# The 2738 pieces of a sparse-attention and SwiGLU kernel issued in another order

## Chip, core and metric

One Trainium2 chip, one of its cores. The time is the device time of one execution in microseconds (us); lower is better. Of the kernel before, three runs and one profiled execution are given.

## What is computed

Block-sparse attention over B=4 sequences, H=8 heads, S=768 positions and D=64, in blocks of 32 positions, followed by a gated feed-forward layer on the 3072 tokens:

```python
mask = np.abs(blk_i - blk_j) <= window            # window = 1
mask = mask | (blk_i == 0) | (blk_j == 0) | (blk_i == n_blocks - 1) | (blk_j == n_blocks - 1)
...
mask[qb * block:(qb + 1) * block, kb * block:(kb + 1) * block] = True   # 3 drawn blocks per row block
scores = np.where(mask, scale * np.matmul(q, k.transpose(0, 1, 3, 2)), -1000000000.0)
attn = softmax(scores); x = attn @ v              # then heads side by side: (3072, 512)
g = x @ w_gate; silu = g * (1.0 / (1.0 + np.exp(-g)))
out = silu * (x @ w_val) @ w_out                  # 512 -> 1536 -> 512
```

So a row block of 32 queries sees its own three neighbouring key blocks, the two edge blocks (first and last) and three blocks whose numbers come from a table in memory. The first and the last row block see all keys.

## The kernel before

The tokens go through in nine chunks (`CHUNKS`): three of 256 tokens, which are batch 0, and six of 384, two for each of batches 1 to 3. The first two chunks run in fp32, the others with every fp32 number split into two fp16 halves and products of three terms. The feed-forward products (L1811 and L1817 into 1536 columns, L1882 back to 512) are most of TensorE's work; attention for later chunks is done between them.

Nothing in the kernel is scheduled by a planner at run time. Every step of the work is a `Task`, made by `Plan.add` with its engine, the tasks that it needs and the buffers that it takes. `Plan.order` walks through the list `TURN` (L48), 2738 task numbers, asserts that each stands behind what it needs, and hands them out in that order; each task then emits its instructions. An engine works through its own instructions in that order and no other. So `TURN` alone decides what an engine does next, and an instruction that waits holds up everything behind it on its engine.

What the prediction speaks of lies in the start-up, on batch 0, whose row blocks go in pairs (`pair0`; "pair 1" below is row blocks 1 and 2, "pair 3" row blocks 3 and 4, and so on: the digit in a tile's name such as `qk_3_0` is the first row block of the pair). For one pair:

- SP's queue loads the table of drawn blocks (L328), three parts of k (L584), three parts of v (L619), the last block of v (L626) and the queries (L1342, L1348). DVE turns the table into numbers (`tables`, L364 to L366 and `rows`, L360). POOL and DVE each load these numbers into registers in pieces of eight row blocks (TENSOR_LOAD, L1111, from `koff`).
- TensorE transposes k (L593); DVE and ACT keep it (L600, L602).
- `keys` copies the drawn key blocks side by side (L1402 and L1404: DVE for the first chunk's two first pairs, POOL for all the other ones), `beside` the neighbouring blocks (L1411, ACT or POOL). Slots are reused, so the copies for a later pair wait until an earlier pair's scores are done.
- the value blocks go into one of six places of `w2all`: the edge blocks by `spread` (L630: one copy on ACT, three on DVE, once for all six places), the neighbouring blocks by `values` (L1429, ACT or DVE), the drawn blocks by `gathered` (L1433: an indirect DMA that POOL issues).
- `scores` on TensorE (L1452, and L1468 for repeated blocks), `top` on DVE (L1474), `power` on ACT (L1484, the exponentials), `turn` on TensorE (L1492), `turned` (L1498, DVE or ACT, to SBUF), `product` with the values (L1512), `scaled` (L1520), `x_turn` (L1529), `x_put` (L1580).

The weights come by SP in pieces (L472) and are decoded on DVE (L450 to L452). In batches 1 to 3 the transposition is a DMA (L1258, `pts<-pp`), and the product is L1270.

Of the kernel before, what the change touches and what calls it, by code (L numbers as in the profile page):

```python
# [48 lines left out]
    2, 60, 7, 5, 0, 6, 18, 1, 3, 129, 23, 303, 22, 16, 21, 36, 28, 29, 84, 219, 38, 4, 8, 9, 19, 40, 20, 10, 14, 11,  # L49
    27, 15, 17, 88, 12, 13, 43, 46, 45, 44, 47, 30, 69, 66, 62, 63, 42, 68, 65, 86, 220, 67, 224, 26, 301, 24, 90,  # L50
    48, 91, 89, 70, 112, 49, 50, 71, 72, 41, 52, 51, 54, 53, 92, 73, 55, 93, 25, 111, 94, 114, 113, 56, 39, 74, 225,
    31, 95, 57, 75, 79, 32, 96, 58, 134, 137, 136, 135, 37, 97, 76, 77, 78, 33, 64, 115, 138, 110, 116, 117, 159,
    158, 80, 98, 139, 157, 160, 81, 140, 118, 100, 120, 119, 141, 142, 124, 99, 179, 85, 182, 102, 87, 107, 221,
    101, 59, 61, 161, 162, 164, 108, 130, 109, 122, 163, 131, 103, 165, 121, 123, 222, 143, 180, 302, 133, 181, 104,
    153, 202, 145, 223, 147, 132, 183, 154, 105, 106, 184, 82, 83, 186, 185, 187, 204, 234, 125, 226, 126, 227, 228,
    203, 235, 144, 146, 166, 127, 229, 201, 230, 205, 309, 148, 168, 206, 149, 188, 308, 128, 447, 155, 208, 156,
    190, 167, 169, 207, 448, 209, 236, 199, 237, 171, 238, 449, 450, 176, 175, 178, 170, 172, 200, 451, 279, 151,
    244, 245, 210, 34, 35, 189, 191, 457, 177, 192, 150, 330, 310, 280, 212, 231, 152, 232, 311, 198, 233, 307, 313,
    197, 239, 312, 173, 193, 214, 240, 194, 281, 174, 458, 211, 213, 215, 314, 283, 282, 246, 247, 195, 216, 248,
    459, 331, 196, 217, 332, 218, 541, 460, 542, 543, 284, 452, 319, 461, 333, 241, 304, 305, 335, 334, 464, 242,  # L60
    466, 249, 250, 315, 467, 336, 317, 316, 243, 465, 468, 269, 337, 327, 462, 306, 463, 318, 544, 285, 545, 471,
    286, 251, 328, 453, 473, 474, 320, 338, 469, 347, 339, 326, 252, 472, 340, 348, 349, 350, 351, 329, 359, 470,
    341, 342, 353, 321, 322, 475, 323, 354, 476, 360, 401, 361, 355, 253, 270, 356, 397, 271, 477, 324, 325, 478,
    364, 362, 366, 357, 343, 480, 481, 254, 370, 365, 272, 546, 344, 400, 367, 551, 479, 273, 368, 371, 372, 553,
    382, 383, 373, 374, 384, 385, 396, 376, 377, 255, 256, 257, 258, 422, 423, 378, 264, 379, 482, 402, 380, 554,
    345, 363, 265, 287, 483, 484, 292, 288, 387, 389, 291, 403, 552, 388, 424, 425, 404, 405, 426, 406, 485, 399,
    390, 486, 555, 289, 487, 391, 266, 684, 407, 267, 556, 557, 1011, 488, 259, 260, 398, 290, 892, 454, 489, 408,
    492, 490, 268, 494, 495, 409, 261, 262, 274, 275, 410, 493, 263, 496, 491, 893, 346, 437, 352, 497, 498, 558,
    559, 560, 561, 562, 565, 548, 566, 547, 438, 276, 896, 293, 277, 278, 411, 439, 298, 432, 572, 563, 564, 567,
# [116 lines left out]
    2669, 2670, 2680, 2681, 2682, 2676, 2677, 2685, 2683, 2686, 2684, 2687, 2688, 2689, 2692, 2693, 2694, 2699,  # L186
    2700, 2695, 2690, 2691, 2696, 2697, 2698, 2706, 2707, 2701, 2702, 2703, 2704, 2714, 2715, 2716, 2708, 2705,
    2709, 2710, 2711, 2712, 2717, 2718, 2720, 2721, 2722, 2719, 2723, 2726, 2724, 2725, 2727, 2728, 2729, 2732,
    2730, 2731, 2733, 2734, 2735, 2736, 2737,
]  # L190


# [1788 lines left out]
```

## Time and profile before

| | |
|---|---|
| runs of before | 756.51, 758.19, 758.41 us; median 758.19 |
| the profiled execution | 756.43 us, of it a span of 754.2 us from the first to the last instruction |
| granted TensorE clock, mean | 0.988 |
| TensorE (PE) | 724.6 us busy, 96% |
| VectorE (DVE) | 546.9 us, 73% |
| ScalarE (ACT) | 471.4 us, 63% |
| GpSimd (POOL) | 236.6 us, 31% |
| chain of work that ended last | PE 80%, DVE 10%, DMA 3%, ACT 2%, issue 2% |

The profile is of one execution. An engine's busy time is the time in which it works on an instruction, its own waits for a port among them; the idle time of the engine that is busy almost throughout is what another order could remove. The granted clock is the share of full speed that TensorE was given.

### The profile page before, as it was taken

The page shows a single profiled execution, that of the slowest core. Times are in us where ns is not written, and L with a number is a line of the kernel's source. Part 1 is how long each engine was busy: PE and PEld are TensorE (multiplying, and loading weights), DVE is VectorE, ACT ScalarE, POOL GpSimd, SP SyncE. Part 2 cuts the span into 40 slices and gives each one's busy share as a digit, 9 for nine tenths or more (in the row PEclk, how much of TensorE's full clock was granted, in tenths as well). Part 3 has the DMA queues.
Part 4 walks back from the last instruction along what each step waited for, and adds up shares of the span by engine and source line. Part 5 has one row for each costly group of instructions (what it writes and reads, how often), then busy time and mean ns, then how long its engine had stood idle before and what let it go on. Part 6 is the DMA issues. An engine that isn't in the chain of part 4 may idle for free.

```text
span 754.2 us, 23313 instructions
## 1 busy us (share of the span) xinstructions
PE 724.6 (96%) x9207; PEld 452.3 (60%) x9207; DVE 546.9 (73%) x1570; ACT 471.4 (63%) x1123; POOL 236.6 (31%) x290
## 2 busy tenths in 40 slices
PE   4779999999999999999999999999999999999998
PEld 3447788884588456645665456645665556545655
DVE  6898999887999988556999677756878466723310
ACT  4698685787878776764887575655766555522221
POOL 3695412132124351220343222321334232302210
PEclk8799999999999999999999999999999999999999
DMA  8656567655799999987899999797758856540001
GB/s 279 193 167 222 174 229 246 203 175 116 186 180 187 183 191 167 192 262 134 189 201 176 219 204 202 184 177 165 168 124 177 165 122 112 92 82 29 0 1 43
DMA packets 182429, 122.91 MB, mean 163 GB/s; under 512 B 131728, under 2 KB 152592, under 8 KB 182320
## 3 DMA queue, kind: packets, MB, share of 16 engines
q1 hardware_dynamic: 176688, 104.12, 60.6%
q0 software_dynamic: 5632, 17.31, 9.6%
q8 instruction: 72, 1.18, 0.7%
q14 instruction: 37, 0.30, 0.1%
HBM read 79.31 MB, written 11.01 MB: 120 GB/s over the span
## 4 chain that ended last, share of the span: by engine, by line
PE 80%; DVE 10%; DMA 3%; ACT 2%; issue 2%; SPq 1%; DVEq 0%; POOL 0%; ACTq 0%; POOLq 0%
PE p L1817 38%; PE po L1882 22%; PE p L1811 9%; PE pv L1270 3%; PE qk L1203 3%; DMA w2all<-in_v_dram,vidx 1%; PE pv L1512 1%; DVE w2all L1429 1%; PE qkf L945 1%; PE pvf L1033 1%; SPq L762 1%; DVE e L1217 1%; DMA pts<-pp 1%; PE qk L1452 1%; DVE w1t L413 1%
## 5 line engine op out<-in xcount | busy, mean ns | idle before, releaser
L1817 PE MATMUL p<-xall,w1t 128*128 128x384 f16 (+1 forms) x2016 | 321.9, 319 | 0.1
L1817 PEld LDWEIGHTS <-w1t 128*128 128x128 f16 x2016 | 193.5, 98 | 118.2 <-issue 5.7
L1841 POOL TENSOR_TENSOR h<-act,h 128x384 f16<-128x384 f32 (+1 forms) x108 | 100.3, 930 | 319.6 <-ACT h L1838 319.3
L1882 PE MATMUL po<-w2all,h 128*128 128x512 f16 (+1 forms) x900 | 191.4, 371 | 1.2 <-issue 1.2
L1882 PEld LDWEIGHTS <-h 128*128 128x128 f16 x900 | 86.4, 98 | 96.6 <-issue 2.3
L1185 POOL DMA_INDIRECT w2all<-vd,vidx x66 | 65.0, 985 | 84.8 <-PE pv L1270 64.2
L1824 ACT ACTIVATE act<-p,gsc 128x384 f32<-128x384 f32 (+1 forms) x84 | 46.8, 559 | 65.5 <-PE p L1817 51.1
L1811 PE MATMUL p<-xall,w1t 128*128 128x256 f32 x384 | 86.6, 384 | 0.4 <-DVE act L1833 0.4
L1838 ACT CAST h<-act 128x384 f16<-128x384 f32 (+1 forms) x108 | 50.7, 470 | 51.5 <-DVE act L1833 51.1
L1828 DVE SCALAR_TENSOR_TENSOR act<-act,p 128x384 f32<-128x384 f32 (+1 forms) x108 | 54.4, 505 | 36.9 <-ACT act L1824 35.8
L1236 ACT ACTIVATE e<-e,mx,es 128x256 f32<-128x256 f32 x132 | 78.2, 593 | 2.2
L1811 PEld LDWEIGHTS p<-xall,w1t 128*128 128x128 f32 x384 | 72.3, 192 | 10.3 <-DVE act L1833 0.7
L1833 DVE SCALAR_TENSOR_TENSOR act<-act,hs,p 128x384 f32<-128x384 f32 (+1 forms) x84 | 49.4, 590 | 14.3 <-PE p L1817 12.2
L413 DVE SCALAR_TENSOR_TENSOR pp<-e,pp 128x512 f16<-128x512 f32 x66 | 48.3, 734 | 10.4 <-ACT pp L410 10.2
L1217 DVE CUSTOM_DVE_ANT_1 e<-qk,msk 128x256 f32<-128x256 f32 x132 | 49.5, 418 | 7.4 <-PE qk L1203 7.4
L1175 DVE COPY kring<-kst 128x256 f16 x198 | 40.2, 256 | 4.2 <-PE qk L1203 2.6
L1755 POOL TENSOR_TENSOR sqx<-sqx 128x768 bf16<-128x768 bf16 (+3 forms) x18 | 22.2, 1232 | 66.9 <-ACT sqx L1751 58.7
L410 ACT ACTIVATE pp<-e 128x512 f16<-128x512 f32 x66 | 40.7, 622 | 3.2 <-DMA pts<-pp 2.8
L1709 ACT ACTIVATE ot<-po,oc 128x512 f32<-128x512 f32 (+1 forms) x25 | 16.3, 659 | 25.8 <-PE po L1882 25.7
L1203 PE MATMUL qk<-kring,qs 64*32 64x256 f16 x1584 | 29.3, 271 | 1.5 <-DVE kring L1176 1.0
L1270 PEld LDWEIGHTS <-pts 128*32 128x32 f16 x2112 | 24.1, 97 | 10.6 <-issue 9.4
L1433 POOL DMA_INDIRECT w2all<-in_v_dram,vidx x22 | 24.5, 1112 | 18.8 <-DVE vidx L360 10.3
(205 smaller groups left out, 917.0 us busy)
## 6 DMA issues: line engine op xcount, KB each, us to landing
stage<-in_w_dram SPq DMA_DIRECT2D x36, 512.0 KB
w2all<-vd SPq DMA_DIRECT2D x66, 192.0 KB
out_dram<-ot SPq DMA_DIRECT2D x19, 256.0 KB
qn<-in_q_dram SPq DMA_DIRECT2D x36, 128.0 KB
stage<-in_v_dram SPq DMA_DIRECT2D x9, 512.0 KB
qraw<-in_q_dram SPq DMA_DIRECT2D x36, 128.0 KB
vd<-stage SPq DMA_DIRECT2D x9, 512.0 KB
stage<-in_k_dram SPq DMA_DIRECT2D x9, 512.0 KB
```

What stands on the lines that cost most here:

```text
L413: nc.vector.scalar_tensor_tensor(lo, src, scale, hi, op0=ALU.mult, op1=ALU.subtract)
L1185: nc.gpsimd.indirect_dma_start(vf[0:96, 1, :], None, bt.vd, bass.IndirectOffsetOnAxis(ap=vidx[0:96, qb : qb + 1], axis=0))
L1203: nc.tensor.matmul(st[g][u * BLK : (u + 1) * BLK], o.q[half, ql, u, col : col + BLK], kg[half, 4 * kl + u].rearrange("p s k -> p (s k)"), ...
L1217: nc.vector.tensor_tensor_reduce(ev[:, g], score_of(g).rearrange("p (s k) -> p s k", k=BLK), o.g.msk[:, qb, :].unsqueeze(2).broadcast_to([ ...
L1236: nc.scalar.activation(ev[:, g], ev[:, g], AF.Exp, bias=nb_[:, g : g + 1], scale=o.g.es[:, 0:1], accum_out=both["rs"][:, n % 2, g : g + 1],)
L1811: nc.tensor.matmul(t[:, 0:tc_], w[:, i + 1, k_ * P : (k_ + 1) * P], x_k(k_), start=k_ == 0, stop=k_ == NKT - 1)
L1817: nc.tensor.matmul(t[:, 0:tc_].rearrange("p (s q) -> p s q", q=BLK), w_[:, f, m, k_, :], x_k(k_, l), start=i == 0, stop=i == 11)
L1828: nc.vector.scalar_tensor_tensor(a_, a_, 1.0, pg.tile[:, 0:tc_], op0=ALU.add, op1=ALU.mult)
L1833: nc.vector.scalar_tensor_tensor(a_, a_, sc, pw.tile[:, 0:tc_], op0=ALU.mult, op1=ALU.mult)
L1838: nc.scalar.copy(hv(f)[:, 0, :], act.tile[:, 0:tc_])
L1841: nc.gpsimd.tensor_tensor(hv(f)[:, 1, :], act.tile[:, 0:tc_], hv(f)[:, 0, :], op=ALU.subtract)
L1882: nc.tensor.matmul(po.tile[:, cs], hv(f)[:, l, ts_], w2h[:, f, m, cs], start=f == 0 and i == 0, stop=f == NF - 1 and i == 2)
```

## The change

Only the list `TURN` differs: the same 2738 numbers, permuted. Its first row before and after (the other rows differ in the same manner):

```diff
 TURN = [
-    2, 60, 7, 5, 0, 6, 18, 1, 3, 129, 23, 303, 22, 16, 21, 36, 28, 29, 84, 219, 38, 4, 8, 9, 19, 40, 20, 10, 14, 11,
...
+    0, 5, 8, 2, 60, 10, 1, 7, 22, 3, 9, 6, 18, 4, 21, 23, 28, 29, 16, 11, 303, 19, 14, 38, 15, 20, 17, 12, 13, 44,
...
```

No instruction is added or taken away but those that set registers and semaphores. Three places of the start-up, as the program has them on their engines:

**SP's first transfers.** Before:

```order
L328 DMA xall<-in_sampled_blocks_dram 128x144
L584 DMA w1t<-in_k_dram 128x2x512 x3
L626 DMA w2all<-in_v_dram 32x512
L619 DMA w2all<-in_v_dram 128x2x512
L1348 DMA q_0_174<-in_q_dram 64x4x128 x2
```

and after:

```order
L584 DMA w1t<-in_k_dram 128x2x512
L328 DMA xall<-in_sampled_blocks_dram 128x144
L584 DMA w1t<-in_k_dram 128x2x512
L619 DMA w2all<-in_v_dram 128x2x512
L584 DMA w1t<-in_k_dram 128x2x512
L1348 DMA q_0_161<-in_q_dram 64x4x128 x2
L626 DMA w2all<-in_v_dram 32x512
```

The table of drawn blocks now stands behind a part of k, the third part of k behind a part of v, and the last block of v behind the first queries.

**DVE and POOL around the first scores.** On DVE, from the copy of the edge values to the first transposed probabilities, before:

```order
L630 COPY w2all<-w2all 32x3x512
L1474 TENSOR_REDUCE mx_1_320<-qk_1_0_271 128x2
L1474 TENSOR_REDUCE mx_1_320<-qk_1_1_272 128x2
L1474 TENSOR_REDUCE mx_3_355<-qk_3_0_326 128x2
L1474 TENSOR_REDUCE mx_3_355<-qk_3_1_327 128x2
L1429 COPY w2all<-w2all 32x512
L1429 COPY w2all<-w2all 64x512
L1498 COPY pts_1_1_373<-pt_1_1_367 128x512
L630 COPY w2all<-w2all 32x3x512
L1474 TENSOR_REDUCE mx_5_406<-qk_5_0_382 128x2
```

and after:

```order
L630 COPY w2all<-w2all 32x2x512
L1429 COPY w2all<-w2all 32x512
L1429 COPY w2all<-w2all 64x512
L1474 TENSOR_REDUCE mx_1_332<-qk_1_0_232 128x2
L1474 TENSOR_REDUCE mx_1_332<-qk_1_1_233 128x2
L1474 TENSOR_REDUCE mx_3_345<-qk_3_0_265 128x2
L1474 TENSOR_REDUCE mx_3_345<-qk_3_1_266 128x2
L1111 TENSOR_LOAD koff
L630 COPY w2all<-w2all 32x3x512
L1498 COPY pts_1_1_395<-pt_1_1_355 128x512
L630 COPY w2all<-w2all 32x3x512
L1474 TENSOR_REDUCE mx_5_422<-qk_5_0_402 128x2
```

The two copies of neighbouring values (L1429) now stand ahead of the tops (L1474), the two larger edge copies (L630) behind them, and a register load that stood far later in the program stands in between. On POOL at the same time, before:

```order
L1111 TENSOR_LOAD koff x3
L1433 DMA w2all<-in_v_dram,vidx 96x512 x6
L1404 REGISTER_ALU
L1404 ISA
L1404 COPY w1t<-kst_233 128x4x32
```

and after:

```order
L1111 TENSOR_LOAD koff
L1433 DMA w2all<-in_v_dram,vidx 96x512
L1111 TENSOR_LOAD koff
L1433 DMA w2all<-in_v_dram,vidx 96x512
L1111 TENSOR_LOAD koff
L1433 DMA w2all<-in_v_dram,vidx 96x512 x2
L1411 COPY w1t<-kst_142 128x4x96 x2
L1404 REGISTER_ALU
```

Four gathers instead of six now stand ahead of the key copies, each of the first three behind a register load of its own. On TensorE the product of pair 1 (L1512, 32 columns of `pv_1`) moved behind the transposes of pair 3 and the scores of pair 7; before it stood ahead of both.

**POOL ahead of the product of batch 0's second chunk.** Before, from the key copies for chunk 2 (`kring`) on:

```order
L1402 COPY kring_104<-kst_233 128x8x32
L1404 REGISTER_ALU
L1404 ISA
L1404 COPY kring_104<-kst_233 128x4x32
L1404 REGISTER_ALU x2
L1404 ISA
L1404 COPY kring_104<-kst_233 128x4x32
L1404 ISA
L1404 COPY kring_104<-kst_233 128x4x32
L1433 DMA w2all<-in_v_dram,vidx 96x512
L1755 TENSOR_TENSOR sqx_909<-sqx_909 128x512
```

and after:

```order
L1433 DMA w2all<-in_v_dram,vidx 96x512 x3
L1755 TENSOR_TENSOR sqx_874<-sqx_874 128x512
L1755 TENSOR_TENSOR sqx_874<-sqx_874 128x256
L1433 DMA w2all<-in_v_dram,vidx 96x512 x2
L1402 COPY kring_104<-kst_142 128x8x32
L1404 REGISTER_ALU
L1404 ISA
L1404 COPY kring_104<-kst_142 128x4x32
```

The gather that stood behind both groups of key copies is now the second of the three in a row ahead of the second group. Further on, the gather that stood behind both additions of squares (L1755) of the next chunk now stands between them. In the rest of the program TensorE's tasks move by at most six places within its own order, and the feed-forward products at the end stay nearly as they were.

## Rows read from the trace of the kernel before

**Rows 1.** Page, busy time, share of the span and instructions.

```profile
PE 724.6 (96%) x9207; PEld 452.3 (60%) x9207; DVE 546.9 (73%) x1570; ACT 471.4 (63%) x1123; POOL 236.6 (31%) x290
```

**Rows 2.** Waits of TensorE: total us, times, longest.

```profile
PE pv L1512 <- DVE pts L1498: 4.1, 1, 4.1
...
PE pv L1512 <- DMA w2all<-in_v_dram,vidx: 2.8, 2, 1.9
```

**Rows 3.** Busy time by stretch: engines (instructions), then clock, DMA share, GB/s.

```profile
0.00:20.00 20.00, 10.19 (x98) 6.41 (x98) 13.92 (x54) 8.82 (x18) 7.56 (x16) 0.83 0.90 284
...
40.00:60.00 20.00, 14.38 (x367) 10.64 (x365) 18.51 (x33) 19.70 (x51) 18.64 (x31) 0.93 0.55 180
...
260.00:660.00 400.00, 397.09 (x5413) 226.29 (x5412) 292.58 (x919) 257.07 (x615) 123.73 (x121) 1.00 0.84 173
```

**Rows 4.** Timeline of DVE, 0 to 37: start, length, idle before in brackets.

```profile
4.55 0.20 DVE L364 SCALAR_TENSOR_TENSOR koff<-xall 128x24 int32<-128x24 int32 x1 [2.52 <-DMA xall<-in_sampled_blocks_dram]
...
12.02 0.69 DVE L630 COPY w2all<-w2all 32x1024 f32<-32x1024 f32 x1
...
16.73 1.22 DVE L630 COPY w2all<-w2all 32x1536 f32<-32x1536 f32 x1
17.88 2.46 DVE L1474 TENSOR_REDUCE mx<-qk 128x2 f32<-128x512 f32 x4
20.36 6.79 DVE L1429 COPY w2all<-w2all 32x512 f32<-32x512 f32 x2
27.19 0.69 DVE L1498 COPY pts<-pt 128x512 f32<-128x512 f32 x1
...
34.01 1.99 DVE L1474 TENSOR_REDUCE mx<-qk 128x2 f32<-128x512 f32 x3 [0.24 <-PE qk L1468]
```

**Rows 5.** Line L1429: ns of one copy, minimum, median, maximum.

```profile
L1429 DVE COPY w2all<-w2all x8: 420/423/6357, 20.4 to 41.3; 32x512 f32<-32x512 f32 x4, 64x512 f32<-64x512 f32 x4
```

**Rows 6.** Timeline of POOL, 7 to 82.

```profile
11.52 1.30 POOL L1433 DMA_INDIRECT w2all<-in_v_dram,vidx  x1 [10.27 <-DVE vidx L360]
...
19.45 0.75 POOL L1404 COPY w1t<-kst 128x128 f32 x3
20.16 0.50 POOL L1411 COPY w1t<-kst 128x384 f32<-128x384 f32 x1
...
25.69 0.76 POOL L1404 COPY w1t<-kst 128x128 f32 x3
...
48.77 2.77 POOL L1404 COPY kring<-kst 128x128 f32 x3
51.70 0.95 POOL L1433 DMA_INDIRECT w2all<-in_v_dram,vidx  x1 [0.16 <-PE pv L1512]
...
71.91 2.24 POOL L1755 TENSOR_TENSOR sqx<-sqx 128x512 bf16<-128x512 bf16 x2 [7.54 <-ACT sqx L1749]
```

**Rows 7.** Lines L1111 and L1433: ns of one register load; us from gather to landing.

```profile
L1111 POOLq TENSOR_LOAD <-koff x3: 1395/1824/2032, 5.2 to 8.8; - x3
L1111 DVEq TENSOR_LOAD <-koff x3: 1857/2097/2905, 5.2 to 185.4; - x3
...
DMA to landing us min/median/max: 3.1/5.5/8.1
```

**Rows 8.** Timeline of TensorE.

```profile
16.20 0.56 PE L1468 MATMUL qk<-dupm,ones_h 128*128 128x192 bf16 x4
...
57.27 1.08 PE L1512 MATMUL pv<-w2all,pts 128*32 128x64 f32 x32 [1.86 <-DMA w2all<-in_v_dram,vidx]
...
79.53 0.99 PE L1512 MATMUL pv<-w2all,pts 128*32 128x64 f32 x56 [0.94 <-DMA w2all<-in_v_dram,vidx]
...
406.11 0.52 PE L1270 MATMUL pv<-w2all,pts 128*32 128x128 f16 x32 [0.39 <-DMA pts<-pp]
```

**Rows 9.** Page, DMA issues: transfer, queue, count, KB each.

```profile
w2all<-vd SPq DMA_DIRECT2D x66, 192.0 KB
```

280 rows, old and new, of the table TURN are left out of this document.

## Prediction

> **What bounds the kernel now.** I read the busy times first. TensorE is busy for 724.6 us of the span of 754.2 [rows 1], so no order can give back more than 29.6 us without making TensorE's own work shorter, and the change adds or removes no work. The table by stretch says where these 29.6 us lie: between 260 and 660 us TensorE is busy for 397.09 of 400, while the first 60 us are far from full, 10.19 of 20 in the first stretch and 14.38 of 20 in the third [rows 3]. The reader is to see there that the third stretch is also one in which ACT works 19.70 and DVE 18.51 of 20: start-up is bound by these two engines and by what they wait for. Then I read TensorE's waits. The largest behind the loading of k is 4.1 us, for the transposed probabilities of the first product, and two waits for gathered values make 2.8 us [rows 2].
>
> The DVE timeline shows the cause of the first. A copy of neighbouring values, 32 partitions by 512, begins at 20.36 and with its sister takes 6.79 us [rows 4]. The same copy takes 0.42 us as a rule, and 6.36 here [rows 5]. On POOL, key copies run from 19.45 to 26.44 without a gap [rows 6], and DVE's copy ends 0.28 us behind them. So such a copy on DVE, from SBUF to SBUF in fp32, stands still as long as POOL goes from copy to copy. The transposed probabilities (27.19) stand behind it. This is the row on which the forecast turns, since the change moves the very copies that can be caught.
>
> **The change, part by part.** All sums are made against the profiled execution, 756.43 us.
>
> *The table behind a part of k.* DVE gets the table's numbers at 4.55 [rows 4]. The table now stands behind a transfer of 512 KB (128 partitions of two rows of 512 fp32). At the 284 GB/s of the first stretch [rows 3] that takes 1.85 us. The table can come later by nothing (if its own latency covers it) up to about 1.85 and one more issue on SP of 0.5, in all 2.3 us. I take 1.1, the middle, because no row shows a small transfer behind a large one. Everything on DVE and POOL that reads the table shifts by this. In return the edge copy of 0.69 us, which stood ahead of the key copies at 12.02, now stands behind them [rows 4]. The key copies thus end 0.4 us later, at 17.15 where they ended at 16.73, and the first scores at 17.2 where they ended at 16.76 [rows 8].
>
> *When POOL begins its key copies.* Before, POOL did three register loads, then six gathers in 7.93 us (11.52 to 19.45), so 1.32 each [rows 6]. After, three loads of 1.82 [rows 7] and four gathers of 1.32 come first: 5.5 and 5.3 us from about 6.3 (the table's 5.2 and the shift), so until 17.1. The slots that the key copies write come free with the first scores at 17.2. POOL starts there, 2.2 us earlier than before.
>
> *DVE's copies meet that run.* DVE does its edge copy from 17.15 to 17.84, and the two copies of neighbouring values want to follow. POOL has asked by then. Does DVE get in? In the row of before it did not, for all the 6.1 us that POOL's run still had. I take the same: POOL's run of two copies of L1411, twelve of L1404 and two of L1411, at 0.5 and 0.25 us each [rows 6], makes 5.0 us, until 22.8. The value copies end at 23.6, and the four tops, 2.46 us [rows 4], at 26.1 instead of 20.34. That is a loss of 5.8 us there, but the product of pair 1 no longer stands in front of the scores that follow.
>
> *The rest of the start-up on DVE.* The register load that came from later in the program takes 2.1 us [rows 7], until 28.2; the edge copy 1.22 [rows 4], until 29.4; the transposed probabilities 0.69 [rows 4], until 30.1. The second edge copy meets POOL's next run, which waits for the scores of pair 5 and the first edge copy, and takes 0.75 for three copies, twice, and 1.0 for two of the others, 2.5 us [rows 6], until 31.9; the copy ends at 33.1. Two tops (half of 2.46) and the small inverses behind them, which I put at 0.3, make 1.5 us, one more copy of probabilities 0.69, and the tops of pair 7 start at 35.3 instead of 34.01 [rows 4]. These tops release ACT's exponentials, and from 40 on ACT has hardly a gap [rows 3]. **+1.3 us**. If POOL lets the copies through at once, the same sum is 5.0 and 1.8 us shorter and the tops start at 28.5 or so: 5.4 us earlier. These are the two ends: −5.4 and, with the table 1.2 us later than I take, +2.5.
>
> The Trainium skill, page "SBUF — State Buffer", section "SBUF: two separate sides", says that DVE and GpSimd share one port pair under a lock which whoever starts first holds for the whole instruction. By that sentence a DVE copy would wait for the one POOL copy under way; the row of 6.36 us shows a wait for a whole run of them, so the measurement is the worse of the two. By the page's lock alone this part would come out near the first rival's −4.4 us; by the row it is the +1.3 above.
>
> *The gather for the second chunk's product.* TensorE waits 1.86 us at 57.27 [rows 8] for a gather issued at 51.70, right behind a group of key copies whose last three took 2.77 [rows 6]. It lands 5.5 us after its issue [rows 7], which is 57.2. Now it is issued ahead of that group, so at least 2.77 earlier, with the shift of 1.3 near 50.2, and lands at 55.7; the product's first half ended at 55.41, where the wait began, and now ends behind that, shifted too. **−1.9 us**; nothing if ACT, which writes the rest of that product's input, turns out to be as late as the gather.
>
> *The gather of the third chunk.* TensorE waits 0.94 us at 79.53 [rows 8]. The gather stood behind two additions of squares that take 2.24 together [rows 6] and now stands behind one, about 1.1 earlier. What is late next is the second addition and the norms that need it, now behind a gather; TensorE's feed-forward products stand ahead of these. **−0.9 us**, bounds −0.9 and +1.3, one gather's worth of delay for those norms.
>
> *The rest.* Between 260 and 660 us TensorE lacks 2.9 us in all [rows 3]. Of these, one product that waited 0.39 us for its transposed probabilities [rows 8] now stands behind one more feed-forward group, which covers it: **−0.4 us**. Moves of up to six places elsewhere I cost at nothing; what hides them is TensorE's queue of feed-forward work. Bounds: −2.9, and a loss that the third rival prices. TensorE's clock I also cost at nothing: it is granted at 0.83 on the mean of the first stretch, so for a part of it at 1.2 GHz, and at the full 2.4 GHz in the long middle [rows 3]; the start-up has idle TensorE time before and after.
>
> *Sum.* +1.3 − 1.9 − 0.9 − 0.4 = −1.9, so 754.5 against 756.43. The three runs and the profiled execution, four times in all, have their middle at 757.35, 0.9 above the profiled one. The same 0.9 on top gives **755.4 us** for a median, against 758.19.
>
> **The rivals.** *The copies get through* (chance 0.25). A copy of DVE that asks at the end of its own copy keeps the port, or waits for one POOL copy. For it: DVE is the one at work when POOL arrives. Against it: the 6.36 us [rows 5]. Four such copies that each wait for one POOL copy of 0.5 us cost 2.0 of the 5.4 us, so the start-up gains between 3.4 and 5.4, say 4.4, and the sum is −4.4 − 1.9 − 0.9 − 0.4 = −7.6: 748.8, and 749.7 for a median.
>
> *ACT and DVE take it all back* (chance 0.16). With 19.70 and 18.51 busy of 20 [rows 3], what the gathers give and what the lock costs may both end in the same queue of work, and the first product of the feed-forward layer then starts when it did. Only −0.4 and a third of −0.9 are left: 755.7, and 756.6 for a median. In effect, nothing changes.
>
> *Slower, by fetches that come late in the long middle* (chance 0.14). In batches 1 to 3 every product needs probabilities that a DMA has transposed, from a queue with a DMA share of 0.84 [rows 3], and one such wait of 0.39 us is all there is now. Where the new order puts one more transfer of 192 KB [rows 9] ahead of such a transposition, it lands 1.1 us later (192 KB at 173 GB/s, rows 3). If that falls once in each of the six chunks on a product with no feed-forward work ahead of it, it costs 6.6 us: +1.3 − 1.9 − 0.9 + 6.6 = +5.1, so 761.5 and 762.4 for a median. It decides as soon as a landing comes later than TensorE's work between; for it speaks that SP's order there is changed nearly throughout, against it that most moves are by two places or fewer.
>
> **How the numbers follow.** My forecast has 0.45. Its own range is 751.8 to 758.5: down by the table's 1.1 and the 2.5 us that the long middle still holds, up by the table's 1.2 and the first gather's 1.9. About 0.3%, 2.3 us, is what a measurement here can tell from no change: 755.9 to 760.5 is the same. Of the forecast's 0.45, 0.27 are below that and 0.18 in it; the first rival lies below (0.25); of the second 0.02 lie below, 0.13 in it and 0.01 above; the third is above. So 0.54 faster, 0.31 same, 0.15 slower. The range, 748.8 to 760.5, takes in the first rival (748.7 to 750.7 by its own bounds) but for its last tenth, and leaves out the third.
>
> **What would show it.** In the profile after: the table's first row on DVE near 5.6; POOL's copies from about 17.3; one or both copies of L1429 near 5 us long, ending where POOL's first run ends, and an edge copy (L630) of about 3 us; the tops of pair 7 near 35; no wait of TensorE above 0.5 us for gathered values at 55 to 60 and at 79. If all copies of L1429 and L630 take 0.4 to 1.2 us, the first rival holds. If TensorE's busy share between 260 and 660 falls below 396 of 400 with waits for `pts<-pp`, the third does. The forecast is wrong if TensorE's idle time in the first 80 us changes by more than 5 us.

## The result, and the profile after

The kernel after takes 750.54 us (median of four executions, 748.77 to 751.29) against 757.88 for four of the kernel before (756.51 to 758.41). The ratio is 0.9908, with a 95% interval of 0.9882 to 0.9934: 7.3 us faster, where 2.8 were forecast (755.4 against 758.19). The time lies in the whole range that was given, 748.8 to 760.5, but below the forecast's own part of it, 751.8 to 758.5, and beside the first rival, 749.7. Four of all executions below, at 848 to 1242 us, fell in a slower state and are left out of medians and ratios.

The profiled execution after is the longest of the four, 751.29 us with a span of 749.1, so the two profiles differ by 5.1 us only. First the busy times of the profile after, and two lines of each page, before and then after:

```profile
PE 721.9 (96%) x9207; PEld 452.3 (60%) x9207; DVE 542.9 (72%) x1570; ACT 473.9 (63%) x1123; POOL 237.0 (32%) x290
...
L1817 PE MATMUL p<-xall,w1t 128*128 128x384 f16 (+1 forms) x2016 | 321.9, 319 | 0.1
L1882 PE MATMUL po<-w2all,h 128*128 128x512 f16 (+1 forms) x900 | 191.4, 371 | 1.2 <-issue 1.2
...
L1817 PE MATMUL p<-xall,w1t 128*128 128x384 f16 (+1 forms) x2016 | 321.1, 319 | 0.0
L1882 PE MATMUL po<-w2all,h 128*128 128x512 f16 (+1 forms) x900 | 190.3, 371 | 0.0
```

Beside [rows 1]: the same 9207 matmuls keep TensorE busy for 2.7 us less, and its idle time falls from 29.6 to 27.2, by 2.4 only. Half of what this pair of profiles differs by is not idle time at all. Most of that half lies in two lines of the feed-forward layer: L1817 is busy for 0.8 us less and L1882 for 1.1 less, though one matmul takes 319 and 371 ns in both. All of it stands behind 100 us, where the granted clock is 1.00. The mean granted clock of the whole rose from 0.988 to 0.998. Busy time by stretch after (engines in the order PE, PEld, DVE, ACT, POOL with instructions, then clock, DMA share, GB/s):

```profile
0.00:20.00 20.00, 10.24 (x94) 6.55 (x94) 12.97 (x53) 8.95 (x15) 7.03 (x19) 1.00 0.90 273
20.00:40.00 20.00, 16.77 (x370) 10.98 (x370) 19.37 (x34) 18.08 (x61) 18.05 (x44) 0.91 0.70 201
40.00:60.00 20.00, 16.09 (x437) 12.01 (x436) 19.45 (x41) 19.67 (x48) 18.06 (x27) 1.00 0.72 223
...
260.00:660.00 400.00, 396.20 (x5369) 226.51 (x5361) 290.04 (x909) 256.15 (x612) 118.44 (x120) 1.00 0.83 172
```

and the second stretch of before, which the rows ahead of the prediction left out:

```profile
20.00:40.00 20.00, 14.49 (x294) 8.87 (x293) 17.94 (x28) 14.18 (x47) 13.51 (x38) 0.83 0.61 172
```

The gain sits in the second stretch, where POOL works 18.05 us instead of 13.51, ACT 18.08 instead of 14.18, and TensorE gets through 370 matmuls instead of 294. TensorE's waits after (total us, times, longest) show that the 4.1 us of [rows 2] are gone, and that other waits stand beside a smaller one for gathered values:

```profile
PE pv L1270 <- DMA pts<-pp: 3.1, 2, 2.5
PE qk L1452 <- ACT w1t L1411: 2.2, 1, 2.2
PE pv L1512 <- issue: 1.7, 1, 1.7
PE pv L1512 <- ACT pts L1498: 1.4, 2, 1.0
PE pv L1512 <- DMA w2all<-in_v_dram,vidx: 1.2, 1, 1.2
PE pv L1529 <- DVE xs L1520: 1.0, 1, 1.0
```

The timeline of DVE (start, length, idle before in brackets) tells why the product of pair 1 no longer waits 4.1 us:

```profile
6.24 0.20 DVE L364 SCALAR_TENSOR_TENSOR koff<-xall 128x24 int32<-128x24 int32 x1 [4.20 <-DMA xall<-in_sampled_blocks_dram]
...
17.58 1.27 DVE L1429 COPY w2all<-w2all 32x512 f32<-32x512 f32 x2
18.89 2.48 DVE L1474 TENSOR_REDUCE mx<-qk 128x2 f32<-128x512 f32 x4
21.40 1.28 DVE L630 COPY w2all<-w2all 32x1536 f32<-32x1536 f32 x1
22.61 0.66 DVE L1498 COPY pts<-pt 128x512 f32<-128x512 f32 x1
...
25.15 2.52 DVE L1501 TENSOR_SCALAR rs<-rs 128x4 f32<-128x4 f32 x1
...
29.21 1.28 DVE L1474 TENSOR_REDUCE mx<-qk 128x2 f32<-128x512 f32 x2
```

and POOL's beside it:

```profile
17.42 1.16 POOL L1411 COPY w1t<-kst 128x384 f32<-128x384 f32 x2 [1.07 <-issue]
18.52 3.09 POOL L1404 COPY w1t<-kst 128x128 f32 x12
21.55 1.42 POOL L1411 COPY w1t<-kst 128x384 f32<-128x384 f32 x2
...
24.12 0.76 POOL L1404 COPY w1t<-kst 128x128 f32 x3
```

POOL's run begins at 17.42, and DVE's two copies of values ask 0.16 us later. In before the two took 6.79 us in such a run [rows 4]; here they take 1.27 together, and the edge copy at 21.40 takes 1.28 in the same run. One instruction is caught later, the small inverse L1501 at 25.15, which takes 0.16 to 0.37 elsewhere in the first 60 us of this profile. The tops of pair 7 begin at 29.21 instead of 34.01.

TensorE's own timeline after:

```profile
28.16 0.54 PE L1512 MATMUL pv<-w2all,pts 128*32 128x64 f32 x24 [1.71 <-issue]
...
50.81 0.88 PE L1512 MATMUL pv<-w2all,pts 128*32 128x64 f32 x48 [0.97 <-ACT pts L1498]
53.62 1.99 PE L1811 MATMUL p<-xall,w1t 128*128 128x256 f32 x8 [0.84 <-ACT pts L1498]
...
58.90 0.99 PE L1512 MATMUL pv<-w2all,pts 128*32 128x64 f32 x56 [1.19 <-DMA w2all<-in_v_dram,vidx]
...
72.74 1.10 PE L1512 MATMUL pv<-w2all,pts 128*32 128x64 f32 x64
...
79.86 0.44 PE L1529 MATMUL pv<-ident,xs 128*128 128x128 f32 x2 [1.03 <-DVE xs L1520]
...
280.21 0.86 PE L1270 MATMUL pv<-w2all,pts 128*32 128x128 f16 x64 [2.46 <-DMA pts<-pp]
```

The product that waited at 57.27 before [rows 8] is the one at 50.81 here, and waits for ACT; the one behind it now waits 1.19 us for its gathered values, at 58.90. The product that waited at 79.53 before is the one at 72.74, without a wait. The first feed-forward product starts at 53.62; before it was at 59.40. From the same places in both timelines, the program after leads by 3.8 us ahead of the product at 50.81, by 6.7 behind it, by 5.8 at the first feed-forward product, by 6.7 behind the product at 72.74, by 5.4 from 100 to 200, by 3.0 behind the wait at 280, and by 5.1 at the end.

The clock, last. Stretches in which it was granted at 0.50, so at 1.2 GHz, in the profile of before:

```profile
12.90:19.70 6.80, 5.28 (x73) 2.11 (x73) 6.45 (x22) 5.09 (x11) 5.34 (x7) 0.50 1.06 349
...
26.60:33.40 6.80, 4.88 (x85) 3.49 (x88) 5.60 (x14) 3.45 (x11) 0.94 (x1) 0.50 0.63 184
...
57.30:60.70 3.40, 3.40 (x41) 2.99 (x42) 2.28 (x15) 3.38 (x7) 2.93 (x7) 0.50 0.88 281
```

and the only one after:

```profile
29.30:32.70 3.40, 3.13 (x37) 1.90 (x38) 3.25 (x8) 3.26 (x13) 2.58 (x7) 0.50 0.66 152
```

17 us against 3.4. Each begins in a gap of TensorE or up to 1.2 us behind it: the gaps are of 2.50, 4.06 and 1.86 us before, 1.71 after. Not every such gap has one: after, the clock is 1.00 behind gaps of 2.20 us (13.06 to 15.26) and 2.46 us (ahead of 280.21). In such a stretch 32 matmuls of a product took 1.08 us (57.27, before [rows 8]); at the full clock 64 of them took 1.10 (72.74, after). It is not this one execution: over four executions of the kernel after the granted clock is 0.997 on the mean, over 29 of the kernel before 0.991, by the clock that is listed for every execution.

### The profile page after: what moved, and what is told of

Same layout as the page of the kernel before. It is cut to its first block, busy times and chain, and to the rows that moved or that the text cites. A ratio compares the mean times of both kernels' runs of the same rounds, so it can differ in the third digit from the quotient of the medians.

```text
span 749.1 us, 23292 instructions
## 1 busy us (share of the span) xinstructions
PE 721.9 (96%) x9207; PEld 452.3 (60%) x9207; DVE 542.9 (72%) x1570; ACT 473.9 (63%) x1123; POOL 237.0 (32%) x290
## 4 chain that ended last, share of the span: by engine, by line
PE 84%; DVE 6%; DMA 5%; issue 2%; POOL 1%; ACT 1%; SPq 0%; DVEq 0%; POOLq 0%
PE p L1817 40%; PE po L1882 24%; PE p L1811 9%; PE pv L1270 3%; PE qk L1203 3%; DMA pts<-pp 2%; DMA w1t<-in_k_dram 1%; PE pvf L1033 1%; PE qkf L945 1%; DVE mx L1474 1%; DMA w2all<-in_v_dram,vidx 1%; DMA w2all<-vd,vidx 1%; DMA ptsf<-ppf 1%; DVE w1t L450 1%; DVE w1t L451 1%
## 5 line engine op out<-in xcount | busy, mean ns | idle before, releaser
L1817 PE MATMUL p<-xall,w1t 128*128 128x384 f16 (+1 forms) x2016 | 321.1, 319 | 0.0
L1817 PEld LDWEIGHTS <-w1t 128*128 128x128 f16 x2016 | 193.7, 98 | 117.3 <-issue 4.7
L1841 POOL TENSOR_TENSOR h<-act,h 128x384 f16<-128x384 f32 (+1 forms) x108 | 101.3, 940 | 331.8 <-ACT h L1838 321.1
L1882 PE MATMUL po<-w2all,h 128*128 128x512 f16 (+1 forms) x900 | 190.3, 371 | 0.0
L1882 PEld LDWEIGHTS <-h 128*128 128x128 f16 x900 | 86.7, 98 | 95.5 <-issue 0.8
L413 DVE SCALAR_TENSOR_TENSOR pp<-e,pp 128x512 f16<-128x512 f32 x66 | 46.3, 708 | 9.2 <-ACT pp L410 9.1
L1755 POOL TENSOR_TENSOR sqx<-sqx 128x768 bf16<-128x768 bf16 (+3 forms) x18 | 21.6, 1199 | 55.2 <-ACT sqx L1751 49.5
L1175 DVE COPY kring<-kst 128x256 f16 x198 | 35.7, 233 | 3.9 <-PE qk L1203 2.6
L1270 PE MATMUL pv<-w2all,pts 128*32 128x64 f16 (+1 forms) x2112 | 29.3, 207 | 4.1 <-DMA pts<-pp 3.1
L1298 ACT CAST x<-x 128x256 f16<-128x256 f32 x33 | 13.2, 399 | 30.9 <-DVE x L1290 30.8
```

What stands on the lines that cost most here:

```text
L1270: nc.tensor.matmul(to[rows_, g, 0:w_], pq[:, g, l, cc, u], vg[:, cc, 0:w_, 2 * u + g, :], start=i == 0, stop=i == 3, tile_position=(0, u * ...
L1817: nc.tensor.matmul(t[:, 0:tc_].rearrange("p (s q) -> p s q", q=BLK), w_[:, f, m, k_, :], x_k(k_, l), start=i == 0, stop=i == 11)
L1841: nc.gpsimd.tensor_tensor(hv(f)[:, 1, :], act.tile[:, 0:tc_], hv(f)[:, 0, :], op=ALU.subtract)
L1882: nc.tensor.matmul(po.tile[:, cs], hv(f)[:, l, ts_], w2h[:, f, m, cs], start=f == 0 and i == 0, stop=f == NF - 1 and i == 2)
```

## Experiments

Each kernel was timed beside the kernel before, on the same chip. Ratios are given with their 95% interval. But for the first two, the edits are moves of single numbers in `TURN`; the medians of before lay between 757.4 and 758.5 us.

**Which part of the list.** The first two kernels cross the two orders: the tasks of one list's first 560 places in that list's own order, all others in the other's, but for a few tasks that move to the seam. The first row of the first of them, beside before:

```diff
 TURN = [
-    2, 60, 7, 5, 0, 6, 18, 1, 3, 129, 23, 303, 22, 16, 21, 36, 28, 29, 84, 219, 38, 4, 8, 9, 19, 40, 20, 10, 14, 11,
+    0, 5, 8, 2, 60, 10, 1, 7, 22, 3, 9, 6, 18, 4, 21, 23, 28, 29, 16, 11, 303, 19, 14, 38, 15, 20, 17, 12, 13, 44,
...
```

> The first 560 entries of the list (about the first 140 us) in the new order, all the rest in the old one. Theory S, the gain is made in the start-up: the tasks of the trace after run 5.4 us earlier at 95 to 180 us, so the whole is 5.4 us faster than before, and without the wait of 2.45 us that the new order has at 277 us it is not slower than the kernel after (749 to 752 us). Theory M, the gain is made by the order in the long middle: no more than 1 us faster than before.

> The reverse: the first 560 entries in the old order, the rest in the new one. Theory S: the middle and the end of the trace after lose 2.4 us at 277 and win about as much back at 516 and 580, so this is within 1 us of before. Theory M: 4 us or more faster than before.

The new start with the old rest took 753.41 us, 0.9941 [0.9915, 0.9967]; the old start with the new rest 757.71, 1.0000 [0.9974, 1.0026]. So the start makes the larger part of the gain, and the rest alone makes none that can be seen. The latter has the same 321.1 and 190.3 us in L1817 and L1882 as the kernel after. The granted clock goes with the start as well: 0.998 over the executions of the first, 0.989 over those of the second. The new start does not bring all of it: its program leads before by 5.8 us at 95 to 140, and then, in its profile, TensorE waits at the seam of the two orders:

```profile
129.64 8.24 PE L1811 MATMUL p<-xall,w1t 128*128 128x256 f32 x37
139.69 1.99 PE L1811 MATMUL p<-xall,w1t 128*128 128x256 f32 x8 [1.81 <-DVE act L1828]
```

This wait stands in neither whole order. Its lead is 3.6 us behind the seam, 2.1 at 220 and 1.2 at the end, so this profile loses as much again in the old rest. By the medians the kernel lacks 2.9 us to the one after, and the two intervals overlap.

**The copies of values.** In the order of before, the two copies of pair 1 (task 41) are put ahead of the tops, as the change has them, and nothing else.

```diff
-    48, 91, 89, 70, 112, 49, 50, 71, 72, 41, 52,
+    41, 48, 91, 89, 70, 112, 49, 50, 71, 72, 52,
```

> The old order with one task moved: the two copies of neighbouring values (L1429) of pair 1 stand on DVE ahead of the four tops, where POOL is still issuing gathers, and not behind them. Theory L, the caught copy alone is the cause: both copies take 0.42 us, the edge copy L630 behind them gets in between POOL's copies as in the trace after, the product of pair 1 starts near 24 instead of 27.93, and the whole is 3 to 5 us faster. Theory P, the next copy is caught in its place (the run of key copies lasts until 26.44): L630 is then 4 to 5 us long, the product starts near 27.7, and the whole gains 0.5 to 1.5 us; the larger part of the gain then needs the product moved behind the scores on TensorE too.

754.99 us, 0.9967 [0.9942, 0.9993]: 2.4 to 2.5 us by the medians and by the ratio. The copies are no longer caught, since POOL's run only begins at 19.83. But the run then catches the edge copy, which now reaches it. DVE's timeline:

```profile
18.12 0.91 DVE L1429 COPY w2all<-w2all 32x512 f32<-32x512 f32 x2
19.07 2.48 DVE L1474 TENSOR_REDUCE mx<-qk 128x2 f32<-128x512 f32 x4
...
22.98 4.94 DVE L630 COPY w2all<-w2all 32x1536 f32<-32x1536 f32 x1
```

and POOL's, whose run of copies ends at 26.84:

```profile
19.83 0.77 POOL L1404 COPY w1t<-kst 128x128 f32 x3
...
26.09 0.76 POOL L1404 COPY w1t<-kst 128x128 f32 x3
```

The rule of [rows 5] thus holds in another place, for another line: the stall moved to the next copy in fp32 that meets the run. It is shorter there, 3.7 us on top of the copy's own 1.2, and the product's second half pays 2.42 of it. That is theory P's mechanism, with a gain above the 1.5 us that it allowed.

So the edge copy (task 25) was put ahead too, which takes all of them out of POOL's way:

```diff
-    48, 91, 89, 70, 112, 49, 50, 71, 72, 41, 52, 51, 54, 53, 92, 73, 55, 93, 25, 111,
+    41, 25, 48, 91, 89, 70, 112, 49, 50, 71, 72, 52, 51, 54, 53, 92, 73, 55, 93, 111,
```

> The old order with two tasks moved on DVE: the value copies (L1429) of pair 1 and the second edge copy (L630) both stand ahead of the four tops, before POOL's run of key copies begins at 19.45, so that none can be caught. Theory L, the caught copy is what the start-up lost: no copy of L1429 or L630 takes over 1.5 us, TensorE's wait of 4.06 us in the first product shrinks to under 1, the tops of pair 7 start 3 to 4.5 us earlier than 34.01, and the whole is 3 to 4 us faster than before. Theory I, TensorE's own instructions then come too late: five of the kernels with the new start-up stand still for 1.2 to 2.2 us at matmul 218 until 28 or 29.5, whatever that matmul is. Here matmul 218 is in the transposes of pair 3 and would be reached near 25.5; by I it starts at 28 or later with no releaser named, the tops of pair 7 are only 1.5 to 2.5 us earlier, and the whole gains 1.5 to 2.5 us.

754.61 us, 0.9969 [0.9942, 0.9996]. Line L1429 takes at most 477 ns and line L630 at most 1216, and the 4.06 us wait of the product is gone. Yet the time is no better than with the copies of values alone, within the intervals. TensorE's timeline says where it went:

```profile
21.59 2.05 PE L1492 MATMUL pt<-ident,e 128*128 128x128 f32 x8 [2.73 <-ACT e L1484]
...
27.59 0.64 PE L1452 MATMUL qk<-w1t,q 64*32 64x256 f32 x11
30.59 1.06 PE L1452 MATMUL qk<-w1t,q 64*32 64x256 f32 x21 [2.37 <-issue]
```

and DVE's, what was late before the first of these rows and what waited for the last:

```profile
19.14 1.21 DVE L630 COPY w2all<-w2all 32x1536 f32<-32x1536 f32 x1
20.28 2.46 DVE L1474 TENSOR_REDUCE mx<-qk 128x2 f32<-128x512 f32 x4
...
31.88 1.29 DVE L1474 TENSOR_REDUCE mx<-qk 128x2 f32<-128x512 f32 x2 [2.41 <-PE qk L1468]
```

The copies now stand in front of the tops, which begin at 20.28 instead of 17.88; the exponentials follow them, and TensorE waits 2.73 us for these at 21.59. So a part of the stall was only moved to an earlier place. Then TensorE stands still for 2.37 us in the middle of a group of scores, with no engine or transfer named as its releaser. The tops of pair 7, free to run on DVE, wait for these scores until 31.88. DVE was no longer the limit there.

The reverse was tried in the order of after: the same two copies behind the tops again (task 41 behind 72).

```diff
-    40, 84, 86, 41, 62, 31,
+    40, 84, 86, 62, 31,
...
-    39, 112, 72, 111, 113,
+    39, 112, 72, 41, 111, 113,
```

> The new order with one task moved back: on DVE the two copies of neighbouring values (L1429) of pair 1 stand behind the four tops again, as before. They then ask near 20.2 us, in the midst of POOL's run of key copies, which ends near 22.3. Theory R, a copy that asks during such a run waits for the whole of it: the first copy takes 2 us or more, the edge copy L630 begins near 23 instead of 21.40, and the whole loses 1 to 2 us against the kernel after. Theory I, it waits for one POOL copy: 0.6 us each as in the trace after, and no change in time.

751.34 us, 0.9909 [0.9874, 0.9943], not to be told from the kernel after. It decides nothing on the copies. The tops themselves came later, so the copies asked at 22.19, where POOL's run was to end at 23.14, and the first of them took 1.23 us: there was hardly a run left to be caught in.

**The gather for the second chunk.** In the order of before the gather (task 156) is put ahead of the group of key copies (task 308).

```diff
-    149, 188, 308, 128, 447, 155, 208, 156, 190,
+    149, 188, 156, 308, 128, 447, 155, 208, 190,
```

> The old order with one task moved: on POOL the gather for the second chunk's product (issued at 51.70) stands ahead of the second group of key copies for chunk 2. My forecast's term: TensorE's wait of 1.86 us at 57.27 goes and the whole is 1.9 us faster. The rival, that ACT and DVE are as late as the gather: less than 0.5 us.

755.89 us, 0.9971 [0.9948, 0.9993]: 1.5 to 2.2 us, by the medians and by the ratio, where the prediction's term was 1.9. The wait of 1.86 us at 57.27 [rows 8] is gone, and the product waits 1.26 us for ACT, as it waited 1.25 for its first half before. TensorE's timeline:

```profile
55.52 1.36 PE L1512 MATMUL pv<-w2all,pts 128*32 128x64 f32 x64 [1.26 <-ACT pts L1498]
...
57.40 1.97 PE L1811 MATMUL p<-xall,w1t 128*128 128x256 f32 x8
```

Then both parts together, all copies ahead and the gather:

```diff
-    48, 91, 89, 70, 112, 49, 50, 71, 72, 41, 52, 51, 54, 53, 92, 73, 55, 93, 25, 111,
+    41, 25, 48, 91, 89, 70, 112, 49, 50, 71, 72, 52, 51, 54, 53, 92, 73, 55, 93, 111,
...
-    149, 188, 308, 128, 447, 155, 208, 156, 190,
+    149, 188, 156, 308, 128, 447, 155, 208, 190,
```

> The old order with three tasks moved: the two of the kernel before this, and the gather for the second chunk's product ahead of the second group of key copies for chunk 2. If these places carry the start-up gain of the new order, the whole is as fast as the kernel with the first 560 entries of the new order, 4 to 5.5 us faster than before; if the many other moves carry it, no more than 2.5 us.

754.13 us, 0.9946 [0.9915, 0.9978]. By the medians and by the ratio these are 3.6 to 4.1 us in one kernel, where the parts alone make 4.5 to 4.6: nearly additive, within the intervals. Three moved numbers out of 2738 give about half of the change, within an interval that goes from a quarter to nearly all of it. They give it at the clock of before, 0.991 over this kernel's executions.

**The other half.** What is left is 3.6 us between this kernel and the one after, and 3.9 to the kernel with both small moves below, timed beside it; the intervals overlap a little. It shows early: in its profile this kernel is 0.3 us behind before at 45 us, where the kernel after leads by 3.8. Of its waits until then, 2.78 us is for the exponentials behind the late tops, where the kernel after waits 0.58 (at 20.23): there the large edge copies stand behind the tops. No run moved them alone. The product of pair 1 (task 57) stands further back on TensorE in the change, so the next try moved it back, with the tasks that have to follow it, in the kernel with all copies and the gather ahead.

```diff
-    31, 95, 57, 75, 79, 32, 96, 58, 134, 137, 136, 135, 37, 97, 76, 77, 78, 33, 64, 115, 138, 110, 116, 117, 159,
-    158, 80, 98, 139, 157, 160, 81,
+    31, 95, 75, 79, 32, 96, 134, 137, 136, 135, 37, 97, 77, 115, 57, 76, 33, 78, 64, 138, 116, 117, 58, 159,
+    158, 80, 98, 139, 157, 160, 110, 81,
```

> The kernel e11_copies_and_gather (old order, value and edge copies ahead of the tops, one gather earlier) with TensorE's product of pair 1 also behind the transposes of pair 3 and the scores of pair 7, as in the new order; its scaling on DVE, one gather on POOL and the next copy into the same buffers follow it. Theory P, this move is the larger part of what is still missing to the new order: the standstill at matmul 218 then falls into the product, which nobody waits for at once, the tops of pair 7 start near 29 instead of 32.4, and the whole is 2 to 3.5 us faster than e11 (750.5 to 752). Theory C, the missing part is spread over the many other moves and the clock: within 1 us of e11 (753 to 755).

755.34 us, 0.9965 [0.9939, 0.9990]: nothing gained. DVE's next copy of probabilities now stands behind the product that was moved back, as DVE's timeline shows:

```profile
30.91 0.69 DVE L1498 COPY pts<-pt 128x512 f32<-128x512 f32 x1 [3.37 <-PE pv L1512]
...
32.66 0.69 DVE L1474 TENSOR_REDUCE mx<-qk 128x2 f32<-128x512 f32 x1
```

In the order of after the product was moved the other way, ahead of the transposes of pair 3, as before had it (task 57 ahead of 75):

```diff
-    56, 33, 75, 95, 135, 137, 96, 136, 97, 134, 77, 115, 160, 57, 157,
+    56, 33, 57, 75, 95, 135, 137, 96, 136, 97, 134, 77, 115, 160, 157,
```

> The new order with one task moved back: on TensorE the product of pair 1 stands ahead of the transposes of pair 3 and the scores of pair 7, as before. Theory P, this move was a part of the gain: TensorE then waits for the edge copy that ends at 24.52, the transposes of pair 3 start near 25.7 instead of 23.17, and the whole loses 1 to 2.5 us against the kernel after. Theory L, the caught copy was all of it: within 0.5 us of the kernel after.

752.32 us, 0.9922 [0.9884, 0.9959]. The tops of pair 7 come at 30.84 and the first feed-forward product at 55.6, so 1.6 and 2.0 us later than in the profile after. Some 0.9 us of this was there before the product: the copies of values begin at 18.52 instead of 17.58. By the medians the kernel is 1.8 us slower, which the intervals do not separate from none. So the place of the product is at most a part, and only inside the whole order. No single move was found that makes the second half. Nor does the higher clock bring it by itself: the new start with the old rest, at 0.998, took 753.41 us, and the three moved numbers, at 0.991, took 754.13, not to be told apart. The second half was seen only with the new start and the new rest together; what in them makes it stays open.

**Two small things that the change got worse.** The table's load (task 2) put back ahead of the first part of k (task 5), and the small inverses of pair 1 (task 56) put behind the run of POOL that caught one; each alone, then both. The two moves, in the order of after:

```diff
-    0, 5, 8, 2, 60,
+    0, 2, 5, 8, 60,
...
-    301, 37, 220, 56, 33, 75,
+    301, 37, 220, 33, 75,
...
-    118, 158, 64, 80,
+    118, 158, 64, 56, 80,
```

> The new order with one task moved back: SP issues the table of drawn blocks ahead of the first part of k, as before. My forecast's first term: DVE gets the table 1.7 us earlier, near 4.55, the first scores end 1 to 1.7 us earlier, and the whole gains 0.5 to 1.7 us against the kernel after, unless POOL's earlier start catches the copies of L1429 again, which would cost 1 us or more. The rival: k's first part lands as much later, and nothing changes.

> The new order with one task moved: the inverse of pair 1 (L1501, L1502), whose first instruction took 2.52 us at 25.15 until POOL's run ended at 27.64, stands behind the value copies of pair 3, near 31 us. It is needed only by the scaling at 34.5. Theory R, it was caught by the run: the second top of pair 5 starts 2.5 us earlier, near 25.2, L1501 takes 0.15 to 0.2 us, and the whole gains 1 to 2.5 us against the kernel after. The rival, that ACT's queue from 30 us on takes it back: less than 0.5 us.

> The new order with two tasks moved: the table of drawn blocks ahead of the first part of k, and the inverse of pair 1 behind the value copies of pair 3. An attempt at a faster order than both. If the table's 1.7 us and the caught inverse's 2.5 us were on the path, 1 to 3 us faster than the kernel after (747.5 to 749.5); if TensorE's instructions at matmul 218 set the pace there, no difference beyond 1 us.

With the table first: 749.18 us, 0.9888 [0.9849, 0.9928]; DVE has the table at 5.24 instead of 6.24, but the first part of k is then late, and TensorE's first transposes start at 6.90 instead of 4.55. With the inverses later: 750.40, 0.9895 [0.9855, 0.9935]. With both: 750.23, 0.9910 [0.9884, 0.9935]. None differs from the kernel after by more than the intervals. In the second of them, by DVE's timeline, the inverse is no longer caught, and the next copy of probabilities waits all the same, because the product on TensorE stands still in front of it:

```profile
29.86 0.69 DVE L1498 COPY pts<-pt 128x512 f32<-128x512 f32 x1 [2.54 <-PE pv L1512]
```

So removing the 2.52 us of L1501 gained nothing that can be seen. No version that was run beats the kernel after by more than its interval.

## Why the forecast was right in sign and too small

*The table behind a part of k.* 1.69 us later (6.24 against 4.55), 1.1 taken, 2.3 the bound. Right in kind. Putting it back brought nothing that can be told from zero: the table came 1.0 us earlier, and the first transposes of k 2.35 later. The step had looked at the table alone.

*When POOL begins its key copies.* 17.3 forecast, 17.42 measured.

*DVE's copies meet that run.* This is the step that failed, +1.3 us. It took the one row of 6.36 us for a rule, that DVE's copy stands still for as long as POOL goes from copy to copy. The copies met the run as foreseen, 0.16 us behind its start, and got through: 0.62 and 0.64 us each. The edge copies took 1.28 and 1.22, and the register load ran at 19.71 to 21.12 beside the tops and cost nothing, where 2.1 were added. The tops of pair 7 came at 29.21; the step said 35.3, and its other end, if the copies get through, 28.5. (By the step's own terms POOL's run, 5.0 us from 17.2, ends at 22.2 and not at 22.8, so it should have said 34.7.) The first rival held, but for its "wait of one POOL copy" for each: up to 0.2 us was added to each copy, and one inverse that no step named was caught for 2.52.

The Trainium skill, page "SBUF — State Buffer", section "SBUF: two separate sides", says that DVE and GpSimd share a port pair, locked by whoever starts first until its instruction ends. The additions of up to 0.2 us in the kernel after agree with it. The waits of 6.36, 4.94 and 2.52 us here go beyond it, since in each of them several of POOL's instructions began and ended while DVE's stood still. For the forecast this means that the row was real but held for its own order: the copies were held in all three profiles with the old order there, and got through in all seven with the new start. A chance of 0.25 for the first rival was too low beside one single row. That the time lies in the whole range is owed to this rival, to which the range had been drawn out, and not to the step.

*The gather for the second chunk.* −1.9, and 1.5 to 2.2 measured alone. Right. In the kernel after the lead grows over that product from 3.8 to 6.7 us; the next product's own gather, which the step did not look at, then takes 1.19 at 58.90.

*The gather of the third chunk.* −0.9, made and given back. The wait is gone, and the lead grows over that product from 6.1 to 6.7 us. Then TensorE waits 1.03 us for DVE's scaling (L1520) at 79.86, and the lead is 5.4 from there on. The step looked for what was late next at the norms; it was DVE's own queue.

*The rest.* −0.4, not seen. TensorE works 396.20 of 400 between 260 and 660 us, 0.9 less than in [rows 3], with one wait of 2.46 us for transposed probabilities at 280. That is the third rival's mechanism, once. It is not shown to be the order's: the five experiments with this same order there have between 395.23 and 398.78, and in these no wait for transposed probabilities is over 1.0 us, and the kernel with only the gather moved, whose long middle is in the order of before, loses some 4 us at 280 to 300.

*The clock, costed at nothing.* The runs neither confirm this nor put a price on it. TensorE does work in the half-speed stretches, 13.56 us of it in before (5.28, 4.88 and 3.40) and 3.13 after, and a matmul there takes twice as long: 1.08 us for 32 of L1512 against 1.10 for 64. But 1.9 of the 2.7 us by which its busy time fell lie in L1817 and L1882, outside these stretches, and the kernel with the old start and the new rest has the same busy times in these two lines without a gain. Nor does the time go with the clock from kernel to kernel. The profile with the product put back (task 57 ahead of 75) has no half-speed stretch and a span of 748.3 us; the one with the table first has 10.2 us of them in its start-up and 745.8, and over its executions that kernel has 0.9945, less than the 0.9972 of the kernel after, and no longer time. Among 93 executions of before, 33 with a clock of 0.988 or 0.989 and 14 with 0.995 both have a mean of 757.2 us. Within the executions of each kernel, 218 in all, 0.01 less of the clock goes with some 2.7 us more on a straight line through them (±1.1). That would make some 1.6 us of the 0.006 between before and after, an estimate, which cannot tell whether the clock or the gap ahead of it costs the time.

*The sum.* The first rival's −4.4 for the start-up (3.8 of lead ahead of the second chunk's product) and the −1.9 came nearly true, the −0.9 and the −0.4 did not stay. The rival's sum was 749.7, and the median is 750.54. That these two lie so close is in part luck, since two of the rival's four terms were lost and the waits at 58.90 and 79.86 stood in none of them.

*What would show it.* POOL's copies from 17.3: right. No wait over 0.5 us for gathered values: right at 79, wrong at 55 to 60, by the next pair's 1.19. Copies of 5 us and tops near 35: wrong. TensorE's idle time in the first 80 us changed by 3.7 us, less than the 5 that were named as the mark, while the step on which the forecast turned was wrong. It was a poor mark: 1236 matmuls ran in these 80 us instead of 1119, so the idle time of the same stretch is not that of the same work, at which the program leads by 5.4 us.

## What to carry to other kernels

A stall that shows in one row of one execution is one outcome of a meeting of two engines; when a change makes the same two meet again in another order, give the case in which it does not happen a chance near even, and look for the order in which they need not meet. When a copy is moved out of a stall, follow the next instruction that meets the same run, and the next queue that its consumer stands in: here, the stall went from one line to the next, then to TensorE's waits for what stood behind the moved copies. And before a change in the mean clock or in the busy time is taken for a cause, see in which lines and stretches the busy time fell, and whether other kernels with that clock are as fast.

## What the runs showed that was not expected

**The same meeting, with and without a stall.** A DVE instruction from SBUF to SBUF in fp32 that asks while POOL copies back to back was held to the end of POOL's run in the profiles of before (6.36 us), of the old start with the new rest (6.35), of the gather alone (6.38) and of the copies alone (4.94). In the kernel after and in the six others with its start, the same copies took up to 0.8 us more than alone, and in the kernel after POOL's own became longer: the pair of L1411 at 21.55 takes 1.42 instead of 0.95. The inverse L1501 of 128x4 asked 0.32 us into one of POOL's L1411 copies in three profiles; it took 2.52 us in the kernel after and 0.66 in the two others, here DVE's row with the product put back ahead of the transposes in the new order:

```profile
26.07 0.66 DVE L1501 TENSOR_SCALAR rs<-rs 128x4 f32<-128x4 f32 x1
```

Copies from PSUM (L1498, up to 0.72 us) and tops of PSUM (L1474, up to 0.71) were never held in these profiles. What decides between the two outcomes stays open.

**TensorE stands still at the same count.** In the kernel after, and in nine others, TensorE pauses for 1.1 to 2.4 us behind 218 or 219 matmuls from the start, at 26 to 29 us, whatever comes next: a product in the kernel after (1.71), a group of scores with all copies ahead (2.37) and with the product put back in the new order (1.52). The profile names no releaser but "issue" in nine of the ten (with the copies back it names the tops, L1474). TensorE reaches that matmul at 30.5 us with the copies of values alone and at 32.5 to 32.7 in before and two others, and does not pause. A second pause of this kind, 0.3 to 2.2 us, stands near 420 us behind 5446 to 5449 matmuls in twelve of the fourteen profiles, with 1.21 in before and 0.85 in after. That the places go by the count speaks for the supply of instructions to TensorE; no run took that supply away or changed it, so this is argued and not shown. In the start-up the pause now stands where the stall on DVE stood.
